# Another written-out order of issue, and another choice of copy engine, in a fused attention, gating and expert kernel

## The chip, the cores and the metric

The kernel runs on one core of a Trainium2 chip. The metric is the device time of one execution in microseconds (us). A core has five engines that each work through an instruction stream of their own, in order: TensorE (PE, with its weight loads shown apart as PEld), VectorE (DVE), ScalarE (ACT), GpSimd (POOL) and SyncE (SP), whose stream here holds the loads. They wait for each other by semaphores.

## What is computed

Three layers follow each other, all in 32-bit floats, for a batch of 2 with 768 tokens, 8 heads of 64 and a model width of 512.

```
attention:  chunks of 32 queries see 16 keys to the left, 8 to the right and 8 memory keys
            a = softmax(q k^T / 8);  x = a v                      -> x[b, s, 512]
gated MLP:  h = gelu(x w_in);  u, v = halves of h
            v_n = (v - mean) / sqrt(var + 1e-6) * g_ln
            v_s = w_sg v_n + b_sg          (over tokens, 768 x 768)
            x1 = x + (u * v_s) w_out
experts:    logits = x1 w_gate; a token takes its argmax expert e, or keeps the expert of
            the token before it, by a second gate
            out = softmax(logits)[e] * relu(x1 w1[e]) w2[e]       (8 experts, 512 x 1024)
```

## The kernel before

The product of two 32-bit matrices is made of three TensorE passes over a high and a low part of each operand (`PASS`, L355), so every operand is split: `split_hi` (L182) is a rounding copy on ScalarE or VectorE, and `split_lo` (L188) a subtraction on VectorE. Attention's own products are plain 32-bit ones.

The work up to the experts consists of small named steps. `at(name, fn)` (L1337) registers them; most are Python generators, and each `yield` ends one piece. `ORDER` (L44 to L98) is a list of 1,021 step names, and the loop at L1440 goes through it: each time a name appears, the next piece of that step is issued. Each engine then executes its own instructions in exactly that order, because the list runs under `manual_schedule` with all five engines. So the list is five queues at once: TensorE's, VectorE's, ScalarE's, GpSimd's, and SyncE's queue of loads. An engine whose next instruction has to wait holds up all that stands behind it.

Step names and their pieces, for batch b and token tile i (128 tokens):

- `lq` loads q and two k tiles (256 KB and two of 192 KB), `q` scales q on ScalarE, `s` makes the scores on TensorE (two mask products, L387, and 32 small ones, L395). `masks` loads the mask rows and builds the mask operands on VectorE (L158 to L171).
- `a..0` takes the row maximum on VectorE (L412), then four exponentials on ScalarE (L415) in two pieces; `a..2` transposes on TensorE (L422) and copies the result out of PSUM (L178 or L180).
- `lv0..`/`lv1..` (three digits) load v (195 KB); `p` multiplies by it (L443), then three VectorE pieces normalise (L451, L453, L456).
- `t` transposes x for 256 tokens and 4 heads (L472), then a high copy and a low subtraction.
- `lv0` to `lv3` (one digit), `lu` and `lo` load the weights w_in and w_out, which arrive as 64-bit floats (two loads of 256 KB each), and `cv`, `cu`, `co` convert them by some nine VectorE pieces each (class `Conv64`, L208; the first, the absolute value, is on ScalarE, L219, or VectorE, L221); `ls`, `cs` do it for w_sg.
- `v`: the matrix product with the v half of w_in (L538, 12 matmuls of 512 columns), gelu, statistics, normalisation and split of one token tile. `u`: the same for the u half (L585). A `v` step of the first batch needs all four `cv` and the `t` steps of its 256 tokens.
- `g..h0` and `g..h1`: the two halves of the token-mixing product (L614), each in two pieces, which fill one PSUM tile `vsp`. `g...1` reads that tile in two pieces (L627) and makes the gated operand. Where `g...1` stands in the list before the last piece of `h1`, TensorE must let VectorE finish that read before it writes the tile on.
- `x`: the product with w_out (L1022) and the addition of x (L1032), stored to DRAM by ScalarE's queue. `lx` and `lg` make the router's logits, `r0` to `r7` and `R..` are the routing of the two batches (some sixty small operations on VectorE in a chain), `RS` gives the places (L942), `G0` to `G2` gather tokens, `XL` builds the first expert tile.
- `consts2` loads small constants: `wgx` in 64-byte rows, `rc`, `g_ln` one number at a time, and `b05`, a row repeated over 128 partitions (393 KB). VectorE then makes eight small operations from them. `rx` makes twelve more. `consts1` is the identity matrix.

`ENG` (L100) gives, for each copy, "a" for ScalarE or "d" for VectorE: AT the copies of `a..2` (24 letters, tile by tile), CB the absolute values and CH the high parts of the 12 weight tiles (cv 0 to 3, cu 0 to 3, co 0 to 3), XH those of `t`, VH of `v`, GH of `g`, SH of w_sg.

All tiles in SBUF come from one pool of 94 slots, and PSUM has eight banks; a new tile waits for the last use of the one whose place it takes. The experts after the list (`moe.run`, L1445) are made of loops whose order for TensorE and SyncE is written out too.

Of the kernel before, what the change touches and what calls it, by code (L numbers as in the profile page):

```python
# [59 lines left out]
lx00.1 s14 a140.0 cu3.0 a120.2 cu2.1 v01.1 a120.2 cu3.0 ls1 lv100 cu3.1 cu3.1 cu3.1 a121.0 v03.0 cu1.1 cu1.1  # L60
cu2.1 cu2.1 cu2.1 a140.0 cu0.1 cu0.1 a121.0 lx01.0 lx01.1 cu3.1 ls4 cu1.1 cu1.1 cu1.1 v03.0 a141.0 cu2.1
a140.0 lv111 v00.1 a130.0 v00.1 ls3 v00.1 a131.2 v02.0 v02.0 lo1 v02.1 a141.0 a130.0 cu2.2 cu0.2 cs7.0 cu2.3
lo3 a131.2 a141.0 cu1.2 v05.0 a140.2 a130.2 a140.2 a141.2 a141.2 cu3.1 v04.0 v03.1 v02.1 lq15 cu1.3 cu0.3 p141
v05.0 v05.1 cu3.1 p111 v03.1 a130.2 lv120 ls0 cu3.2 v03.1 p141 p141 p111 p111 v04.0 p111 v01.1 p110 cu3.3 p140
p141 v04.1 co3.0 v01.1 p100 u02.0 lv101 v01.2 v04.1 p110 v02.1 p110 u02.0 q15 p110 p100 v03.1 v03.1 u02.0 p140
p140 v03.1 v02.1 u02.1 s15 a151.0 a150.0 u00.0 u00.0 p100 ls5 v00.1 v04.1 p140 lv150 p100 v03.1 v03.2 a150.0
v05.1 v04.1 a121.2 a121.2 a150.0 a150.2 a150.2 v05.1 u03.0 v04.1 a151.0 a151.0 u00.0 p121 lv130 v04.1 v04.1
ls8 cs8.0 p101 co2.0 u00.1 p120 p121 p121 p120 lo0 co0.0 v04.2 u00.1 p130 p131 p130 v01.2 p121 p130 u03.0
v02.1 p120 p130 cs6.0 cs6.1 u02.1 u03.0 u03.1 u03.1 lv151 u01.0 u01.0 lx02.0 lx02.1 v00.1 co2.0 v04.2 u02.1
t100 v02.1 u03.1 a151.2 cs8.1 u04.0 v05.1 p120 v00.1 p101 p101 v00.2 v00.2 v05.1 v05.1 v05.1 v01.2 v04.2 cs1.0  # L70
p101 u05.0 v02.1 t100 t100 u05.0 cs7.1 v00.2 a151.2 p151 p150 cs1.1 v02.2 u00.1 p131 u01.0 v02.2 p150 p150
cs5.0 v02.2 u04.0 v05.2 cs4.0 co0.0 v03.2 v03.2 p131 co3.0 g04h0 ls2 g05h0 v05.2 cs3.0 v05.2 p131 cs4.1 co2.1
co2.1 g04h0 g04.1 g04h1 p150 cs5.1 g04h1 cs0.0 t111 cs0.1 cs3.1 co3.1 g05h0 g05h1 g05.1 cs2.0 u04.0 t111 cs2.1
g04.1 u04.1 u04.1 g05h1 g05.1 t111 g01h0 co2.1 co2.1 u04.1 p151 g04.1 g02h0 t101 g00h0 g00h0 co0.1 p151 co1.0
g02h0 u05.0 co0.1 u05.1 p151 g02h1 g01h0 g01h1 g02h1 t110 co1.0 u05.1 co0.1 co0.1 co0.1 co0.1 co2.1 g03h0
co2.1 co2.2 co2.3 t110 g00h1 co1.1 co3.1 co3.1 t101 t101 v11.0 g01h1 u05.1 t121 t110 g03h0 co1.1 co1.1 co1.1
t120 g03h1 g03h1 u01.1 u01.1 t121 co1.1 co1.1 u01.1 co3.1 g05.1 g01.1 g01.1 g01.1 co0.2 t121 g04.1 co0.3 co1.2
g01.1 g00h1 v11.0 co1.2 v11.1 co0.2 co0.3 g04.1 co3.1 co3.1 g00.1 v12.0 v12.0 g00.1 t120 t120 g00.1 g00.1
g03.1 g03.1 v12.1 v11.1 v12.1 v12.1 v11.1 v13.0 v11.1 v11.1 v11.1 v13.0 v13.1 co1.3 v10.0 v11.1 v15.0 v15.0
v12.1 v12.1 v13.1 v13.1 co3.2 g03.1 v14.0 co3.3 g02.1 g01.1 g02.1 v15.1 v15.1 v14.0 g02.1 u12.0 v12.1 v12.1  # L80
co3.2 v10.0 co3.3 u15.0 u15.0 lx12.0 lx12.1 v10.1 v10.1 v15.1 u12.0 v14.1 v15.1 v10.1 v11.2 v12.2 u12.0 v13.1
v15.1 v15.1 v15.1 u13.0 u13.0 v14.1 v14.1 u11.0 v11.2 v11.2 co0.4 u13.0 v13.1 v13.1 u12.1 co2.2 u13.1 u12.1
co0.4 g05.1 g05.1 g00.1 lx10.0 co3.4 co3.4 co2.3 co2.4 co2.4 v10.1 v12.2 v12.2 u10.0 v15.2 co1.3 co1.4 g02.1
g02.1 v10.1 v10.1 v10.1 v14.1 u14.0 g03.1 u15.0 u13.1 g03.1 u10.0 u10.0 u13.1 v10.2 v10.2 co1.4 u11.0 v10.2
lg01.0 u10.1 lg01.1 v14.1 v14.1 zero lg02.0 lg02.1 u11.0 u11.1 u11.1 u12.1 v14.1 lg00.0 v15.2 v15.2 lx10.1
x02h0 x02h1 g15h0 v14.2 v14.2 u14.0 v13.1 g12h0 u10.1 v13.2 v13.2 x02.1 lg00.1 v14.2 v13.2 u11.1 u10.1 g12h0
g12.1 g13h0 g15h0 r0 r0 r0 g13h0 g12h1 u14.0 u14.1 u14.1 g12h1 g15.1 g12.1 g13.1 g11h0 g11h0 g13h1 g12.1 g11h1
r1 u15.1 u14.1 u15.1 r1 r1 r1 g15h1 g14h0 g12.1 r1 g15h1 r1 r2 g14h0 r2 r4 r5 r5 g11h1 u15.1 g15.1 r2 g15.1
x04h0 r5 r5 g12.1 r5 g10h0 pre0 g13h1 g13.1 g13.1 g13.1 g15.1 g10h0 x01h0 r5 x01h1 g15.1 g15.1 g15.1 g11.1
# [1447 lines left out]
```

## Time and profile before

| | us |
|---|---|
| median of 3 runs | 446.39 |
| lowest and highest | 442.04, 447.13 |
| the profiled execution, device time | 445.0 |
| its span, from the first to the last instruction | 443.0 |

Around the span lie 2.0 us. In the span TensorE is busy 412.4 us (93%), its weight loads 361.2 (82%), VectorE 338.6 (76%), ScalarE 207.5 (47%) and GpSimd 43.1 (10%). The page and the trace name an instruction by line, engine, operation and tiles, written as result<-operands. "Idle before" is the time in which the engine stood still just before an instruction, and the arrow names what ended it. Matmuls overlap each other: one of 256 columns lasts 281 ns in the rows but the next starts well before it ends, so a group's mean duration is not what it costs; its busy time is a union of the intervals. The same holds, in a smaller way, for VectorE and ScalarE.

### The profile page before, as it was taken

Reading aid. Unit: us, or ns where it says so; the run is one execution under the profiler, and the core shown is the slowest. Engines: PE = TensorE matmul, PEld = TensorE weight load, DVE = VectorE, ACT = ScalarE, POOL = GpSimd, SP = SyncE. Lnnn points to the kernel's source line nnn. Section 1 sums busy time; section 2 is a strip of 40 time slices with the busy share of each in tenths; the row PEclk is TensorE's granted clock in tenths of the full one; section 3 lists DMA queues with packets and bytes.
Section 4 is the critical chain, followed back from the end, with each engine's and each line's share of the span. In section 5 each row is a group of like instructions: output and inputs, shape, how many; then the busy total and the mean of one; then the engine's idle time right before and its main releaser. Section 6 shows DMA issues by size and latency. Waiting matters only on the chain. (4 is left out here: it accounts for less than half of the span.)

```text
span 443.0 us, 9234 instructions
## 1 busy us (share of the span) xinstructions
PE 412.4 (93%) x3317; PEld 361.2 (82%) x3317; DVE 338.6 (76%) x800; ACT 207.5 (47%) x453; POOL 43.1 (10%) x55
## 2 busy tenths in 40 slices
PE   2887999999999999999799889999999999999991
PEld 1666788998998999998678779889889889988981
DVE  2688999998995889657688997968696696796900
ACT  3696777644232262111020357636656574474510
POOL 1000000110000011000000323001121120000101
PEclk9989999999999999999999999999999999999997
DMA  7999997200000000002705399999897797540101
GB/s 213 307 304 275 319 258 213 80 26 1 1 1 0 1 1 0 2 1 95 277 32 204 112 354 392 391 354 369 250 368 245 256 331 266 189 150 0 44 24 39
DMA packets 43117, 74.74 MB, mean 169 GB/s; under 512 B 6003, under 2 KB 13047, under 8 KB 43066
## 3 DMA queue, kind: packets, MB, share of 16 engines
q1 hardware_dynamic: 38938, 63.87, 44.4%
q0 software_dynamic: 2400, 7.08, 4.5%
q10 hardware_dynamic: 1728, 3.15, 1.9%
q8 instruction: 28, 0.46, 0.4%
q14 instruction: 23, 0.19, 0.1%
HBM read 67.78 MB, written 7.08 MB: 169 GB/s over the span
## 5 line engine op out<-in xcount | busy, mean ns | idle before, releaser
L189 DVE TENSOR_TENSOR we_l<-raw,we_h 128x512 fp32r<-128x512 f32 x160 | 101.9, 688 | 7.1 <-ACT we_h L184 6.1
L184 ACT ACTIVATE we_h<-raw 128x512 fp32r<-128x512 f32 x131 | 73.8, 630 | 15.9 <-DVE s_iw L964 15.4
L1177 PE MATMUL op<-we_h,ht_l 128*128 128x512 f32 x120 | 47.4, 395 | 1.2 <-DVE ht_l L189 1.2
L1177 PE MATMUL op<-we_h,ht_h 128*128 128x512 f32 x120 | 47.8, 398 | 0.0
L1177 PE MATMUL op<-we_l,ht_h 128*128 128x512 f32 x120 | 47.2, 394 | 0.0
L614 PE MATMUL vsp<-sg_h,vh_h 128*128 128x256 f32 x144 | 41.6, 289 | 4.8 <-DVE gtmp L627 4.8
L1132 PE MATMUL hp<-xe_h,we_h 128*128 128x256 f32 x160 | 45.4, 284 | 0.0
L1132 PE MATMUL hp<-xe_l,we_h 128*128 128x256 f32 x160 | 44.9, 281 | 0.0
L1132 PE MATMUL hp<-xe_h,we_l 128*128 128x256 f32 x160 | 44.9, 281 | 0.0
L614 PE MATMUL vsp<-sg_l,vh_h 128*128 128x256 f32 x144 | 40.4, 281 | 0.0
L614 PE MATMUL vsp<-sg_h,vh_l 128*128 128x256 f32 x144 | 40.4, 281 | 0.0
L614 PEld LDWEIGHTS vsp<-sg_h,vh_h 128*128 128x128 f32 x144 | 27.1, 188 | 6.4 <-DVE gtmp L627 6.1
L415 ACT ACTIVATE a<-sc,nm 128x96 f32<-128x96 f32 x96 | 25.4, 368 | 10.7 <-DVE nm L412 8.2
L1132 PEld LDWEIGHTS hp<-xe_l,we_h 128*128 128x128 f32 x160 | 30.1, 188 | 0.0
L1132 PEld LDWEIGHTS hp<-xe_h,we_l 128*128 128x128 f32 x160 | 30.1, 188 | 0.0
L1132 PEld LDWEIGHTS hp<-xe_h,we_h 128*128 128x128 f32 x160 | 30.1, 188 | 0.0
L1186 POOL DMA_INDIRECT out_dram<-o,sidx x15 | 15.8, 1050 | 129.9 <-ACT o L1185 109.4
L1177 PEld LDWEIGHTS op<-we_h,ht_l 128*128 128x128 f32 x120 | 22.5, 188 | 6.9 <-DVE ht_l L189 1.6
L585 PE MATMUL ups<-x_h,in_h 128*128 128x256 f32 x96 | 27.8, 289 | 0.0
L525 ACT ACTIVATE th<-sq 128x512 f32<-128x512 f32 x24 | 15.1, 629 | 26.9 <-DVE sq L522 26.8
L614 PEld LDWEIGHTS vsp<-sg_l,vh_h 128*128 128x128 f32 x144 | 27.1, 188 | 0.1
L614 PEld LDWEIGHTS vsp<-sg_h,vh_l 128*128 128x128 f32 x144 | 27.1, 188 | 0.0
(252 smaller groups left out, 999.5 us busy)
## 6 DMA issues: line engine op xcount, KB each, us to landing
raw<-in_w SPq DMA_DIRECT2D x160, 256.0 KB, 5.2
v<-in_vw SPq DMA_DIRECT2D x24, 195.0 KB, 6.0
k<-in_kw SPq DMA_DIRECT2D x24, 192.0 KB, 5.8
raw_in<-in_w_in SPq DMA_DIRECT2D x16, 256.0 KB, 6.4
q<-in_qT SPq DMA_DIRECT2D x12, 256.0 KB, 6.1
x1d<-x ACTq DMA_DIRECT2D x12, 256.0 KB, 2.5
rsg<-in_w_sgT SPq DMA_DIRECT2D x9, 256.0 KB, 6.8
raw_out<-in_w_out SPq DMA_DIRECT2D x8, 256.0 KB, 6.2
```

The costliest lines, as they stand in the source:

```text
L184: nc.scalar.activation(hi, src, AF.Copy)
L189: nc.vector.tensor_tensor(lo, src, hi.bitcast(F32), ALU.subtract)
L415: nc.scalar.activation(self.a[:, j, :], sc[:, j, :], AF.Exp, bias=nm[:, j : j + 1])
L525: nc.scalar.activation(th, self.sq, AF.Tanh, scale=C2)
L585: nc.tensor.matmul(ps[:, i * 256 : (i + 1) * 256], win_u[k][wa][:, f * 128 : (f + 1) * 128], xT[self.b].at(wb, k, 256 * self.g, 256), star ...
L614: nc.tensor.matmul(self.ps[:, h * 256 : (h + 1) * 256], self.vh[s].hl[wa][:, f * 128 : (f + 1) * 128], rhs_sg(wb, s, self.g), start=(s == ...
L1132: nc.tensor.matmul(ps[:, i * 256 : (i + 1) * 256], self.w[f // 4 * 4 + k][wa][:, f % 4 * 128 : (f % 4 + 1) * 128], self.x[k // 2][wb][:, k ...
L1177: nc.tensor.matmul(self.po[c], h[wa][:, o : o + 128], self.w[8 + k][wb], start=(k == 0 and n == 0), stop=(k == 7 and n == 2),)
L1186: nc.gpsimd.indirect_dma_start(out, bass.IndirectOffsetOnAxis(ap=sidx[:, c : c + 1], axis=0), o, None, bounds_check=NT - 1, oob_is_err=False,)
```

## The change

`ORDER` gets another sequence of the same 1,021 names with the same number of pieces each, and `ENG` other letters. No step is added, removed or changed, and the code of the experts is the same. The start and the end of the list, and `ENG`:

```diff
 ORDER = """
-lq01 masks q01 s01 a010.0 a010.0 consts1 a011.0 a011.0 a011.0 consts2 rx lq00 q00 s00 lq02 q02 lq04 q04 s02
-a021.0 a010.0 a011.2 a011.2 a021.0 a021.0 s04 a001.0 a001.0 a020.0 lv2 cv2.0 a001.0 a001.2 lq03 q03 s03 cv2.0
-cv2.1 a020.0 lv3 lv1 a040.0 a040.0 cv2.1 a020.0 a041.0 a040.0 lq10 a000.0 a000.0 a031.0 a031.0 cv2.1 cv2.1
-cv2.1 a041.0 a030.0 cv1.0 a010.2 cv3.0 cv3.0 a041.0 cv3.1 a001.2 a040.2 a031.0 a040.2 cv3.1 a010.2 q10 a030.0
-a041.2 a031.2 cv3.1 cv3.1 cv1.0 lq05 a000.0 cv3.1 cv3.1 cv1.1 lq11 q05 s10 a101.0 a100.0 a030.0 a000.2 a000.2
-s05 a050.0 a030.2 cv1.1 a021.2 lv000 a101.0 a101.0 cv1.1 a051.0 a031.2 a041.2 lv001 q11 s11 a111.0 cv3.2
-a030.2 cv1.1 p000 p000 a021.2 lv010 a050.0 p001 p000 p000 a050.0 lv041 cv2.1 a110.0 cv3.3 lv011 a101.2 a020.2
-a100.0 a100.0 a100.2 lv030 a051.0 a050.2 p001 p001 a020.2 lv031 p001 a101.2 a110.0 a110.0 p010 a050.2 cv1.1
-cv1.1 p010 p041 p030 p010 a051.0 p010 lv040 p041 lv0 p031 cv2.2 p030 lv020 p030 p041 lv021 a100.2 p030 p031
-p011 lv050 cv2.3 p011 p040 p031 t000 cv0.0 lv051 cv0.0 p040 p040 p040 p011 p011 a110.2 lq13 lq12 a051.2 p041
-p031 a110.2 p020 cv0.1 cv0.1 cv0.1 t001 cv0.1 a051.2 p021 p021 p021 p050 p050 a111.0 t001 a111.0 a111.2 lu0
-cv1.2 p021 p050 p050 p051 p020 t011 t000 t020 q13 lu2 p051 p051 p051 cv0.1 cv0.1 t001 t020 p020 p020 t020
-cv0.2 cv0.3 lq14 a111.2 s13 t021 q12 t000 t010 s12 cv1.3 a130.0 cu0.0 lu1 t011 v01.0 lu3 a121.0 a120.0 t010
-t010 a120.0 a131.0 cu2.0 t011 v01.0 v01.1 lv140 lo2 cu0.0 cu0.1 cu0.1 cu0.1 a131.0 v01.1 v01.1 v01.1 cu1.0 ls6
-t021 cu0.1 t021 a120.0 v00.0 q14 lv121 lv110 cu1.0 ls7 cu1.1 cu2.0 lx00.0 a131.0 lv131 lv141 cu2.1 v00.0 v00.1
...
-g11.1 g11.1 g10.1 g11.1 g10h1 g10h1 r5 g13.1 lg11.0 g11.1 g10.1 g10.1 g10.1 g10.1 pre1 r5 pre2 pre3 x13m0 r6
-x01.1 r6 r6 r6 r6 g14.1 r1 r1 x13m1 g14h1 x13m2 r6 x13m3 lg10.0 g15.1 g14h1 lx11.0 x12m0 g14.1 r6 g14.1 g14.1
-g14.1 lg10.1 lx11.1 x11m0 lg11.1 lg12.0 x12m1 r7 x12m2 lg12.1 x13.1 r3 r5 R1 R1 R1 x05h0 cm0 cm1 x04h1 x04.1
-x02.2 R2 R2 R2 R2 R2 x11m1 x11m2 x05h1 x00h0 R2 R2 R3 R3 R3 x12m3 x12.1 x05.1 RM RA RP x00h1 x03h0 RA x03h1 RP
-RP x01.2 x11m3 RP cm2 RP RP x00.1 RP RP RP RP RA RA RA x03.1 R2 x10m0 RP x10m1 x13.2 x10m2 x10m3 RA RA x04.2
-x00.2 x12.2 RA x11.1 RA x03.2 x11.2 RA x10.1 x14m0 x14m1 RP RP RP RP RP RA RP RP RP RP x14m2 x14m3 RP RP RZ RP
-x15m0 x15m1 RP x15m2 RZ x15m3 R4 RL x05.2 x10.2 RP x14.1 RP G0 RP x15.1 RS RS RE RT RP RT RO RT RT RT x14.2 RE
-XL g15.1 x15.2 G1 cm3 XL XL RA XL G2
+masks lq04 q04 lq03 q03 lq02 q02 s04 a040.0 a040.0 a040.0 s03 a031.0 lq05 q05 a030.0 s02 a041.0 a031.0 a031.0
+a020.0 consts1 a020.0 a020.0 s05 a030.0 a031.2 a050.0 a041.0 a041.0 a021.0 a030.0 lq01 q01 a031.2 a030.2
+a030.2 a020.2 a020.2 lv020 a021.0 a021.0 s01 a010.0 a021.2 a041.2 lv3 cv3.0 cv3.0 lq00 a021.2 p020 q00 cv3.1
+cv3.1 lv1 a050.0 a051.0 a050.0 a050.2 a010.0 a010.0 a041.2 cv3.1 cv1.0 cv1.0 lv2 a051.0 a011.0 a051.0 lv030
+cv3.1 a011.0 lv021 s00 a000.0 a050.2 a010.2 cv2.0 p030 a011.0 cv2.0 lv011 a001.0 cv3.1 cv2.1 cv3.1 cv3.2 cv1.1
+a010.2 a011.2 cv2.1 cv2.1 a051.2 lq10 q10 p030 a040.2 lq12 p020 p030 lv010 p030 a051.2 lv031 a000.0 a000.0 lv0
+p021 cv2.1 cv2.1 s10 lq11 a011.2 p011 p021 cv1.1 cv1.1 cv1.1 a001.0 p021 cv1.1 a001.0 p020 q12 a101.0 a000.2
+a000.2 cv1.1 p020 s12 p021 p031 a101.0 a100.0 cv3.3 a040.2 p011 a100.0 a101.0 a101.2 a121.0 a120.0 p010 p031
+a001.2 p031 lv041 a100.0 cv1.2 a121.0 a121.0 p011 p011 a100.2 t010 q11 a001.2 cv0.0 cv0.0 lv001 a100.2 a120.0
+a120.0 cv2.1 lv050 lv000 cv0.1 cv0.1 a101.2 cv0.1 cv0.1 cv0.1 cv0.1 s11 lv040 p031 a111.0 a111.0 p041 p041
+t011 p041 p041 p001 a110.0 cv1.3 cv0.2 cv2.2 t011 p010 p010 t011 p040 p040 p001 p001 p000 p001 p000 cv2.3 p050
+t001 p040 p040 p050 a110.0 p050 p050 a111.0 a110.0 lq13 q13 p010 p000 t010 t010 t001 t001 a111.2 p000 lv051
+s13 a130.0 a110.2 lq14 q14 t020 t020 p051 p051 p051 lu2 a111.2 t000 p051 s14 t020 cv0.3 t000 cu2.0 t000 a110.2
+a140.0 cu2.0 cu2.1 a131.0 a131.0 a131.0 a141.0 a120.2 a140.0 a120.2 consts2 rx t021 t021 v00.0 v01.0 a141.0
+a141.0 a141.2 lv131 lq15 q15 v01.0 t021 v00.0 v04.0 lv111 a131.2 lv141 v01.1 a140.0 a141.2 v01.1 lu1 cu1.0
...
+g14.1 g11h1 g15h0 r1 g15h0 g14h1 x03.2 g15.1 g15.1 g14h1 g15.1 g15h1 g13h0 u11.1 r1 u11.1 u11.1 g11.1 g11.1
+g11.1 r2 g15.1 r2 g12h0 g12h0 x01h0 g14.1 x05h0 g14.1 u12.1 g11.1 g11.1 g14.1 u12.1 g12.1 g13h0 u12.1 g15h1 r1
+r4 x02.2 g10.1 g13.1 g12h1 pre1 g12h1 r5 r5 r5 g13h1 g13h1 r5 r5 r6 r6 g15.1 g15.1 r5 r1 g10.1 r6 r5 r6 g12.1
+x11m0 pre2 r6 pre3 g15.1 x05h1 g15.1 lg10.0 g14.1 lg12.0 r2 g12.1 cm0 g12.1 g12.1 x13m0 r6 g13.1 x10m0 x10m1
+g15.1 lg10.1 g13.1 g13.1 lx11.0 lx11.1 r5 r3 g13.1 r5 lg11.0 lg11.1 r6 x10m2 lg12.1 x05.1 x10m3 r7 R1 R1 R1
+x01h1 x01.1 x13m1 R2 R2 R2 R2 x11m1 x13m2 x00h0 R2 R2 cm1 R3 R3 x00h1 RM RA x10.1 x12m0 x05.2 x10.2 RA RA RA
+x11m2 RA RA RP RP x13m3 RP RP x01.2 RP RP RP cm2 x04h0 R2 x13.1 x13.2 x00.1 x00.2 x11m3 R2 RP RP RP RL x11.1
+x11.2 R3 x04h1 x04.1 x04.2 RP RP RP RP RP x12m1 x12m2 x12m3 x12.1 x12.2 x15m0 x15m1 x15m2 RA RA x15m3 RA RP RP
+RA RA RP RP RZ RZ x15.1 RP RP RP x14m0 RP RP R4 RP RP x14m1 x14m2 x15.2 RP G0 x14m3 x14.1 x14.2 RO RS RE RS RT
+RT RT RT G1 RE cm3 G2 RA XL XL XL XL RT RP
...
 ENG = dict(
-    AT="adddaaaaadaaaaaaadaaaaaa",
-    CB="addaadaaaaaa",
-    CH="aaadaddadadd",
-    XH="aaaaaaadaaaa",
-    VH="daadaadaadad",
-    GH="daadaadddadd",
-    SH="dadaaadad",
+    AT="aaadadddaaaaaaaaaaaaaaaa",
+    CB="ddddaaaaaaaa",
+    CH="aadaaaadadda",
+    XH="aaaaaaaaaaaa",
+    VH="adaaaaadaadd",
+    GH="aaddaaadaddd",
+    SH="aaaadaaad",
 )
```

## Rows read from the trace of the kernel before

**Rows 1.** Windows of the trace, first 51 us: busy PE, PEld, DVE, ACT, POOL; PEclk, DMA, GB/s
```profile
0.00:10.00 10.00, 3.06 (x36) 1.61 (x36) 2.34 (x11) 3.36 (x9) 2.09 (x11) 1.00 0.69 195
10.00:20.00 10.00, 7.73 (x110) 5.24 (x110) 5.35 (x25) 5.10 (x17) 0.00 (x0) 1.00 0.96 299
20.00:30.00 10.00, 8.59 (x126) 5.92 (x125) 8.72 (x23) 9.17 (x36) 0.00 (x0) 0.83 1.06 336
30.00:40.00 10.00, 8.75 (x191) 7.58 (x189) 9.47 (x34) 8.95 (x28) 0.00 (x0) 1.00 1.05 243
40.00:51.00 11.00, 9.16 (x165) 7.09 (x163) 8.96 (x28) 7.64 (x17) 0.00 (x0) 1.00 1.03 341
```

**Rows 2.** Windows, the later stretches, same columns
```profile
0.00:51.00 51.00, 37.30 (x621) 27.43 (x621) 34.84 (x118) 34.22 (x101) 2.09 (x11) 0.97 0.96 284
51.00:90.00 39.00, 38.77 (x424) 33.94 (x421) 38.02 (x101) 26.54 (x71) 2.10 (x3) 1.00 0.71 188
90.00:120.00 30.00, 28.07 (x256) 27.25 (x255) 26.88 (x66) 11.28 (x23) 2.01 (x3) 1.00 0.04 10
120.00:200.00 80.00, 80.00 (x607) 75.40 (x607) 62.87 (x147) 24.54 (x47) 4.46 (x8) 1.00 0.00 1
200.00:260.00 60.00, 54.91 (x358) 44.88 (x357) 48.52 (x158) 13.81 (x29) 6.42 (x6) 1.00 0.46 160
```

**Rows 3.** Tile vps: ns min/median/max, first and last start; timeline row of the second
```profile
L538 PE MATMUL vps<-in_h,x_h x48: 388/393/503, 51.0 to 148.4; 128*128 128x512 f32 x48
...
53.88 0.39 PE L538 MATMUL vps<-in_h,x_h 128*128 128x512 f32 x1
```

**Rows 4.** Waits of TensorE: total us, times, longest
```profile
PE sc L387 <- DVE mind L167: 5.8, 1, 5.8
...
PE vsp L614 <- DVE gtmp L627: 4.8, 4, 2.7
```

**Rows 5.** The page's DMA issues: count, KB each, us to landing
```profile
v<-in_vw SPq DMA_DIRECT2D x24, 195.0 KB, 6.0
...
k<-in_kw SPq DMA_DIRECT2D x24, 192.0 KB, 5.8
...
q<-in_qT SPq DMA_DIRECT2D x12, 256.0 KB, 6.1
...
raw_in<-in_w_in SPq DMA_DIRECT2D x16, 256.0 KB, 6.4
```

**Rows 6.** Timeline from 8 to 13 us: VectorE and ScalarE waiting for loads
```profile
10.79 0.56 DVE L505 TENSOR_SCALAR b<-b 128x768 f32<-128x768 f32 x1 [1.38 <-DMA b<-in_b_sg]
...
11.48 0.63 ACT L381 ACTIVATE q<-q 128x512 f32<-128x512 f32 x1 [1.22 <-DMA q<-in_qT]
```

**Rows 7.** Groups by line and form: busy us, mean ns, idle before
```profile
L395 PE MATMUL sc<-k,q 64*64 64x96 f32 x384 | 13.7, 290 | 3.4 <-ACT q L381 3.3
...
L422 PE MATMUL at<-ident,a 128*96 128x128 f32 x96 | 15.4, 294 | 2.0 <-ACT a L415 1.4 <-DVE xt L456 0.3 <-DVE x_l L189 0.2
...
L412 DVE TENSOR_REDUCE nm<-sc 128x4 f32<-128x384 f32 x24 | 12.6, 552 | 6.4 <-PE sc L395 6.4
...
L189 DVE TENSOR_TENSOR x_l<-xtp,x_h 128x512 fp32r<-128x512 f32 x12 | 8.2, 686 | 3.9 <-ACT x_h L184 3.9
...
L180 DVE COPY at<-at 96x512 f32<-96x512 f32 x5 | 3.4, 677 | 0.4 <-PE at L422 0.4
...
L186 DVE CAST g_h<-gtmp 128x512 fp32r<-128x512 f32 x6 | 2.5, 417 | 0.1
...
L221 DVE TENSOR_SCALAR cv_in<-raw_in 128x256 uint32<-128x256 uint32 x6 | 1.6, 282 | 0.0
...
L672 DVE CAST rtxb<-wgx 128x16 fp32r<-128x16 f32 x4 | 0.7, 167 | 0.0
```

**Rows 8.** Timeline of TensorE around two late waits
```profile
214.00 0.39 PE L614 MATMUL vsp<-sg_h,vh_h 128*128 128x256 f32 x1 [2.68 <-DVE gtmp L627]
...
248.18 0.46 PE L942 MATMUL inv<-s_eqj,m1v 128*128 128x19 f16 x12 [0.53 <-DVE s_eqj L923]
```

More of the change, by code (lines that the diff above doesn't have):

```diff
@@ L60 @@
[L60 to L89, printed above, removed]
@@ new lines @@
+a140.0 cu2.0 cu2.1 a131.0 a131.0 a131.0 a141.0 a120.2 a140.0 a120.2 consts2 rx t021 t021 v00.0 v01.0 a141.0
+a141.0 a141.2 lv131 lq15 q15 v01.0 t021 v00.0 v04.0 lv111 a131.2 lv141 v01.1 a140.0 a141.2 v01.1 lu1 cu1.0
+lv101 cu1.0 cu2.1 cu2.1 s15 a130.0 p111 v00.1 lv100 v01.1 v01.1 v00.1 cu1.1 a130.0 cu1.1 ls0 a140.2 a121.2
+v01.1 cu2.1 cu2.1 a131.2 lv120 a140.2 v00.1 cu1.1 cu1.1 a121.2 a130.2 lu3 cu3.0 a130.2 lu0 v00.1 p101 lv151
+v00.1 v04.0 lx02.0 cu3.0 a151.0 p111 p111 lx02.1 cu1.1 v00.1 a151.0 cu1.1 ls1 p100 p100 lv130 p111 p101 cu1.2
@@ new lines @@
+cu3.1 v04.1 v03.0 cu3.1 p120 cu0.0 lx00.0 cu0.0 p101 a151.0 a151.2 p100 cu0.1 cu3.1 p101 v04.1 v04.1 cu2.1
+v03.0 cu1.3 v00.1 v00.2 cu0.1 cu0.1 cu0.1 cu2.2 lv110 p120 lx01.0 a150.0 lx01.1 ls3 ls2 p110 cu3.1 ls8 cs3.0
+cu3.1 v02.0 lx00.1 v03.1 v03.1 p110 p110 p110 p100 cu0.1 cu0.1 lv121 cu3.1 t101 v05.0 v03.1 t101 cu2.3 a150.0
+cu0.2 v05.0 t100 a150.0 t101 cu0.3 p131 cu3.2 cu3.3 p130 p130 p131 cs8.0 p130 p130 a151.2 p121 ls5 lo1 v04.1
+v04.1 v04.1 lv150 p131 u00.0 u00.0 ls4 v01.1 v02.0 p121 p121 lo3 p120 p120 p121 v02.1 v03.1 v01.1 v01.2 co3.0
@@ new lines @@
+co1.0 cs1.0 lo2 lv140 u03.0 v00.2 p131 co2.0 v04.1 u00.0 v02.1 v03.1 cs4.0 v02.1 v05.1 lo0 u05.0 co2.0 cs4.1
+u03.0 v05.1 ls7 cs7.0 u00.1 ls6 a150.2 a150.2 u03.0 u05.0 v05.1 v05.1 p150 co0.0 p151 cs8.1 u03.1 u01.0 v02.1
+t100 u03.1 u00.1 p151 u03.1 v00.2 cs6.0 v03.1 p151 t100 p150 p150 p150 u01.0 u04.0 v03.1 cs3.1 co1.0 co2.1
+co3.0 p151 u04.0 u04.0 v03.2 v02.1 v01.2 p140 p141 p140 v03.2 v04.2 p140 p141 u05.0 u00.1 u02.0 v02.1 co3.1
+v11.0 co1.1 co1.1 v02.1 v05.1 v05.1 u01.0 u02.0 co1.1 v04.2 cs7.1 v05.1 v05.2 v02.2 p141 p141 v10.0 cs2.0
@@ new lines @@
+cs2.1 co2.1 v02.2 cs5.0 v05.2 cs6.1 v01.2 v02.2 g05h0 p140 v03.2 g04h0 v05.2 v04.2 g04h0 cs0.0 v10.0 v10.1
+g04.1 v10.1 v10.1 v10.1 co0.0 cs0.1 v11.0 g05h0 g05h1 cs1.1 u04.1 g04h1 g04h1 v11.1 u04.1 u04.1 g00h0 co1.1
+zero v10.1 cs5.1 u02.0 g01h0 g04.1 g01h0 co0.1 co2.1 co2.1 g04.1 g03h0 g03h0 g03h1 co1.1 co1.1 g01h1 co0.1
+co3.1 u01.1 co0.1 g04.1 g04.1 g00h0 g05.1 v11.1 co3.1 v11.1 v11.1 u01.1 co2.1 u01.1 g00h1 co3.1 g02h0 g00h1
+g02h0 co1.2 co0.1 co1.2 u05.1 u05.1 g05h1 g00.1 g00.1 g05.1 u05.1 g05.1 v10.1 co0.1 co0.1 co1.3 g02h1 u02.1
@@ new lines @@
+g01h1 t120 g01.1 t110 g01.1 g03h1 t110 co0.2 t110 co0.2 v10.1 g05.1 v10.2 g03.1 g02h1 u02.1 u10.0 g03.1 u02.1
+co3.1 t121 t121 co0.3 co0.3 t111 g03.1 t111 g00.1 u10.0 t111 t120 v12.0 t120 t121 v15.0 v12.0 co2.1 co2.2
+v12.1 co2.3 v12.1 v12.1 v11.1 g05.1 u11.0 v15.0 v15.1 v15.1 v15.1 v13.0 v12.1 g00.1 v13.0 v15.1 v13.1 v14.0
+v13.1 v11.1 v12.1 co1.3 g02.1 g02.1 g03.1 g02.1 g02.1 v13.1 v13.1 co3.1 g00.1 lx12.0 co2.2 g01.1 co3.2 v11.1
+v10.2 v12.1 v11.2 co3.3 v15.1 v15.1 v15.1 v14.0 v14.1 v14.1 g01.1 u14.0 v12.1 lx12.1 v10.2 g03.1 u14.0 co0.4
@@ new lines @@
+u15.0 u15.0 v11.2 v11.2 g02.1 co2.3 u11.0 v15.2 co3.2 co0.4 co3.3 lx10.0 u14.0 x02h0 u14.1 x02h1 u13.0 u13.0
+v15.2 lx10.1 x02.1 u14.1 v14.1 u15.0 v14.1 u15.1 u15.1 v13.1 x03h0 u15.1 g01.1 v12.2 v12.2 u14.1 x03h1 v12.2
+v13.1 v13.1 v14.1 v14.1 v13.2 co3.4 co1.4 co1.4 v14.1 co2.4 g11h0 co2.4 x03.1 u12.0 u10.0 v13.2 u10.1 u10.1
+v14.2 v14.2 u13.0 co3.4 u10.1 g14h0 v15.2 lg00.0 u12.0 v13.2 v14.2 g14h0 lg01.0 lg01.1 u13.1 u13.1 g10h0 g10h0
+g10.1 lg02.0 g11h0 lg02.1 lg00.1 pre0 r0 r0 u13.1 u11.0 g10h1 g10h1 r0 r1 u12.0 g11h1 r1 g10.1 g10.1 r1 r1
```

## The prediction

> **What bounds the kernel now.** I read the windows first, then the waits of TensorE, then the list itself. In the windows look at the PE column against the length of each window. From 51 to 90 us TensorE is busy 38.77 of 39, from 120 to 200 all of 80 [rows 2]. Nothing that only reorders work can gain there, since the same matmuls remain. What is left to gain is its idle time: 51.00 - 37.30 = 13.7 us before 51 us, 30.00 - 28.07 = 1.9 from 90 to 120, and 60.00 - 54.91 = 5.1 from 200 to 260 [rows 2], 20.7 us in all. 51.0 us is where the first large product, of a v step, starts [rows 3]; from there TensorE always has a store of large products.
>
> Before that point three resources share the blame. VectorE is idle 12.3 of the first 20 us (20 - 2.34 - 5.35), then busy 27.15 of the 31 us that follow (8.72 + 9.47 + 8.96) [rows 1]. The DMA share is 1.03 to 1.06 from 20 us on, at 243 to 341 GB/s, but 0.69 at 195 GB/s in the first ten [rows 1]. TensorE starts only at 5.8 us, when VectorE has built the mask operand [rows 4]. The first 20 us starve all engines; afterwards VectorE and the loads run nearly full.
>
> **The start of the list.** At present the loads of `consts2` stand behind the first q, so VectorE waits for `b05` until 10.79 us and the second q is scaled only at 11.48 [rows 6]. In the new list `masks` comes first of all, then q and k of tiles 4, 3, 2, 5, 1; the weights begin after 3,402 KB, and `consts2` comes behind 11,947 KB. What this gives is worked out from three sides.
>
> Loads: by the sizes [rows 5] I add up the list. Now, up to the last scores in front of the first v product (`s12`): ten tiles of q and k, 6,400 KB, twelve v, 2,340, six weight halves, 3,072, and constants, 592: 12,404 KB. After, up to `s14`: eleven tiles, 7,040, twelve v, 2,340, four weight halves, 2,048, the mask, 7: 11,435 KB, or 11.7 MB. At about 300 GB/s, the level of the windows from 10 us on [rows 1], that is 39 us. Starting after about 2 us, the last k lands near 41 and the v product can start at 43 to 44, after `s14` and six transposes. This is the lower end.
>
> TensorE: eleven score steps and 17 transposing steps instead of ten and 16 lie ahead of the first v product. One score step is 13.7 / 12 = 1.14 us, one transposing step 15.4 / 24 = 0.64 [rows 7], so 1.8 us of its work moves from behind that point to before it, into time now idle.
>
> VectorE: it has done 34.84 us of work by 51 us [rows 2]. For the same point the new list needs three more row maxima (12.6 / 24 = 0.53 each), four more absolute values, as CB puts all of cv on VectorE (1.6 / 6 = 0.27 each), and two more subtractions (8.2 / 12 = 0.68): +4.0. The operations of `consts2` and `rx` move behind it: `b05` 0.56 [rows 6] and three kinds at 0.7 [rows 7], -2.7. So 36.1 us of work. Its idle time in the first 20 us falls, as five tiles of attention are ready by then: ten maxima, 5.3, three copies of AT at 0.68 (the four d of the new AT all lie early), 2.0, the masks, about 1, and the start of cv3, about 1.5, make 9.8 us of work, so 10.2 idle instead of 12.3. From 20 us to the v product it had 3.9 idle [rows 1]; I take 2, as loads of weights come later but attention is further ahead. 36.1 + 10.2 + 2 = 48.3 us. VectorE is then the last of the three, ahead of the loads (44).
>
> So the v product starts at 48.3 instead of 51.0, 2.7 us earlier, with 1.8 us more done: 4.5 us.
>
> A rule about the constants: the windows show 195 GB/s in the first ten microseconds and 299 in the next [rows 1]. The Trainium skill (DMA: Bandwidth & Descriptors, Why small descriptors are slow) says that each descriptor costs a fixed overhead, which tells most on short ones; by it the 64-byte and 4-byte rows of `consts2` are slow wherever they stand, and moving them back only moves the loss to a time when the queue is full. By that rule 10 x (1 - 195 / 299) = 3.5 us of transfer time would fall on `lv131`, `lq15` and `lu1`, and the sum would be unchanged as long as TensorE has the first two v products; if instead the slow start is just the queue filling, the first 20 us stay as starved as now and the sum is 2 us smaller.
>
> **Behind the first v product.** `consts2` now makes VectorE wait in mid-list for `b05`. Behind it stand `rx`, the subtraction of `t021` and the gelu of v. Loads take about 6 us to land [rows 5], and with the queue full this one can be late too. TensorE has v00 and v01 in front of anything that needs `t021`'s subtraction: the first product now starts at 51.0, the second at 53.88 [rows 3], so two are 5.8 us of cover. I cost the wait at nothing, between 0 and 3 us.
>
> The letters: 31 d become 24. AT and XH lose one each from PSUM (0.68), CH two, VH one, GH one and SH two from SBUF (0.42 each), CB gains one weight tile of two pieces (0.28) [rows 7]: -1.4 - 2.5 + 0.6 = -3.3 us on VectorE, and about as much more on ScalarE, which is busy 11.28 of 30 us and less from 90 us on [rows 2]. So VectorE runs some 3 us further ahead in the middle. The 1.9 us idle there, where it was busy 26.88 of 30 [rows 2], should mostly go: -1.5 us, between -1.9 and +2.
>
> The end: the same pattern that costs 4.8 us now, TensorE waiting to write `vsp` on until VectorE has read it [rows 4], is there in seven products of the old list and in seven of the new one. The longest, 2.68 us [rows 8], came of rank operations in VectorE's queue. The routing chain of the second batch starts (`R1`) with 90 matmuls of `x` left now and 84 in the new list, and TensorE waits for its end 0.53 us now [rows 8]. Six matmuls are half a product of 2.9 us, 1.4 us less cover; but `cm0` with two weight subtractions, 0.69 each like those of [rows 7], leaves the chain. I cost the end at nothing, between -3 and +4. The experts are the same.
>
> Sum on the profiled execution: 445.0 (span 443.0 and 2.0 around it) - 4.5 - 1.5 = 439.0. The median of the three runs is 1.4 above that execution, so I forecast 440.4.
>
> **Rivals.** (A) VectorE is not last and the loads decide: v starts at 44, 7.0 us earlier, plus 1.8, plus 1.5 to 3 later: 10.3 to 11.8, 434.6 to 436.1. For it: VectorE's pieces for the weights can fill every gap. Against: it ran 27.15 of 31 us already. (B) The start is gained but waits later take it back: all seven `vsp` reads late at 4.8 / 4 = 1.2 us each, 8.4 instead of 4.8, and 2 us for `b05`: 440.4 + 5.6 = 446.0, no change. For it: large products that come earlier find VectorE less far; against: its queue is shorter. (C) Slower: VectorE decides and is held up ahead of the first v product. cv0, the last weight, comes in one piece behind its load (8,345 KB into the list, 31 us at 300 GB/s), and everything of attention behind it waits. If VectorE's idle time before the v product is not 12.2 but 20 us, v starts at 56.1, 5.1 us later, less 1.8: 449.7. It decides from 52.8 us on (51.0 + 1.8), that is from 16.7 us of idle time, against 16.2 now. (D) The order does nothing, as TensorE's idle time merely sits elsewhere: that is B's number.
>
> **How the numbers follow.** The forecast 0.50, A 0.25, B (with D) 0.16, C 0.09. The likeliest gives 440.4. The range goes from 432.5, two microseconds below A, to 448.5, most of the way to C. A measurement of this kernel can tell about 2% (8.9 us) from no change: below 437.5 lie nearly all of A and a few hundredths of the forecast, 0.26; above 455.3 only the tail of C, 0.04; within, 0.70.
>
> **What would show it.** Right: the first v product (L538) at 46 to 50 us; VectorE idle about 10 us in the first 20; TensorE's first instruction near 4.5 us; idle time of TensorE before the v product down from 13.7 to about 9; the window from 120 to 200 still full. Wrong: a v product after 52 us, a wait of several microseconds at L505 with TensorE idle behind it, or new waits of `vsp` or of L942 above 5 us together.

## The result, and the profile after

The changed kernel takes 440.37 us (median; 437.00 to 441.79) where the kernel before took 446.76 beside it: ratio 0.9883, 95% interval 0.9837 to 0.9930. Timed again later it takes 438.64 against 444.30: 0.9859 (0.9812 to 0.9906). So it is about 6 us faster (5.7 and 6.4 by the medians), 1.2 to 1.4%. The profiled execution took 441.71 us with a span of 439.9, 3.1 us less than before.

The windows of the changed kernel, with the columns of [rows 1] and [rows 2]:

```profile
0.00:10.00 10.00, 4.95 (x68) 3.15 (x68) 1.65 (x7) 3.90 (x8) 1.17 (x9) 1.00 0.76 242
10.00:20.00 10.00, 8.55 (x151) 5.85 (x144) 7.02 (x16) 9.29 (x35) 0.00 (x0) 1.00 1.07 348
20.00:30.00 10.00, 7.59 (x89) 5.61 (x91) 7.90 (x26) 7.17 (x24) 0.98 (x2) 0.68 1.04 267
30.00:40.00 10.00, 9.30 (x190) 7.34 (x192) 9.32 (x31) 7.56 (x25) 0.00 (x0) 0.98 1.00 257
40.00:51.00 11.00, 9.24 (x165) 7.30 (x168) 9.54 (x30) 7.22 (x19) 0.00 (x0) 0.84 0.95 261
0.00:51.00 51.00, 39.65 (x647) 29.26 (x650) 35.42 (x106) 35.14 (x106) 2.15 (x11) 0.90 0.96 275
51.00:90.00 39.00, 38.14 (x373) 32.78 (x362) 35.29 (x111) 26.32 (x69) 1.75 (x3) 1.00 0.75 207
90.00:120.00 30.00, 30.00 (x276) 28.53 (x275) 26.36 (x64) 12.64 (x25) 2.23 (x3) 1.00 0.00 1
120.00:200.00 80.00, 80.00 (x603) 76.17 (x602) 61.78 (x142) 24.67 (x46) 4.71 (x8) 0.98 0.06 18
200.00:260.00 60.00, 57.48 (x389) 47.90 (x389) 52.33 (x166) 16.50 (x34) 6.31 (x6) 1.00 0.46 161
```

Read the first column after the length. TensorE's idle time fell from 13.7 to 11.35 us in the first 51, from 1.9 to 0 between 90 and 120, and from 5.1 to 2.5 between 200 and 260; 51 to 90 lost 0.6. That is 6.2 us less idle time, but the span fell by only 3.1. The difference stands in the PEclk column: 0.90 over the first 51 us against 0.97, and 0.98 from 120 to 200 against 1.00. A busy TensorE at half clock is not a gain. By that column the clock took back up to 5.2 us (0.07 of 51 and 0.02 of 80), and the spans say 3.1: such a sum gives an upper bound.

TensorE's waits, to be read against [rows 4] (total us, times, longest):

```profile
PE sc L387 <- DVE mind L167: 3.1, 1, 3.1
PE xp L443 <- DMA v<-in_vw: 2.4, 1, 2.4
PE xp L443 <- DVE x_l L189: 1.4, 1, 1.4
...
PE ups L585 <- DVE xt L456: 0.9, 1, 0.9
...
PE inv L942 <- DVE s_eqj L923: 0.7, 1, 0.7
```

The wait for the mask came down from 5.8 to 3.1. The waits for `vsp`, 4.8 us before, are in no row at all: the pattern of [rows 8] is gone. Two early waits, for a load of v and for a subtraction, are new.

The first v product (tile vps, as in [rows 3]) and the operation on `b05` that [rows 6] showed waiting, with first and last start:

```profile
L538 PE MATMUL vps<-in_h,x_h x48: 387/394/502, 52.0 to 151.5; 128*128 128x512 f32 x48
```

```profile
L505 DVE TENSOR_SCALAR b<-b x1: 558/558/558, 53.7 to 53.7; 128x768 f32<-128x768 f32 x1
```

v starts at 52.0, not at 48.3 as forecast, and later than the 51.0 of before. L505 has no wait: moving the constants back cost nothing here. The windows show 242 instead of 195 GB/s in the first ten microseconds and 261 instead of 341 from 40 to 51. The Trainium skill (DMA: Bandwidth & Descriptors, Why small descriptors are slow) gives each short descriptor a fixed cost, and these two rates fit that. They do not show it: the loads of `consts2` are issued from 42.2 to 44.2 us here, but the rate is 257 from 30 to 40 us already, and the kernel before has 243 there without these rows [rows 1]. No engine waited for them.

The stretches where the clock fell, TensorE alone (length, busy, PEclk, DMA share, GB/s):

```profile
22.00:24.00 2.00, 0.00 (x0) 0.92 1.09 277
24.00:26.00 2.00, 1.78 (x20) 0.50 1.00 305
26.00:28.00 2.00, 2.00 (x10) 0.50 1.02 251
28.00:30.00 2.00, 2.00 (x23) 0.50 1.01 287
...
44.00:46.00 2.00, 2.00 (x14) 0.54 0.93 229
...
174.00:176.00 2.00, 2.00 (x10) 0.50 0.00 0
```

0.50 is the lower of the two levels, 1.2 of 2.4 GHz. From 22 to 24 us TensorE waited for v; behind that wait it worked at half clock up to about 30 us. So three questions: is the early part worth what was forecast, where does the rest of the gain come from, and what do the letters do?

### The profile page after: what moved, and what is told of

Read it like the earlier page. It is cut to its first block, busy times and chain, and to the rows that moved or that the text cites. A ratio compares the mean times of both kernels' runs of the same rounds, so it can differ in the third digit from the quotient of the medians.

```text
span 439.9 us, 9222 instructions
## 1 busy us (share of the span) xinstructions
PE 416.3 (95%) x3317; PEld 364.9 (83%) x3317; DVE 335.5 (76%) x794; ACT 211.0 (48%) x459; POOL 43.0 (10%) x55
## 5 line engine op out<-in xcount | busy, mean ns | idle before, releaser
L585 PE MATMUL ups<-x_l,in_h 128*128 128x256 f32 x96 | 27.2, 284 | 0.0
```

The source lines that it names most:

```text
L585: nc.tensor.matmul(ps[:, i * 256 : (i + 1) * 256], win_u[k][wa][:, f * 128 : (f + 1) * 128], xT[self.b].at(wb, k, 256 * self.g, 256), star ...
```

## The experiments

Ratios are to the kernel before, timed beside each kernel. Four kernels have other line numbers: in the two that splice the lists near the first v product, and in the two that change the order or the engines alone, every line named is one less.

**Order and engines apart.** The first keeps the new `ORDER` with the old `ENG`, the second the reverse.

```diff
-    AT="aaadadddaaaaaaaaaaaaaaaa",
-    CB="ddddaaaaaaaa",
+    AT="adddaaaaadaaaaaaadaaaaaa",
+    CB="addaadaaaaaa",
...
```

> New order of issue, old choice of engines (31 copies on VectorE instead of 24). My theory: the order carries most of the gain and the choice of engines about 1.5 us, by about 3 us less work on VectorE between the first v product and 120 us. So this kernel gains 4 to 5 us against the kernel before (ratio about 0.990), and TensorE idles about 2 us more between 51 and 120 us than in the changed kernel. Rival: the choice of engines matters as much as the order; then this one gains under 2.5 us (ratio above 0.994).

442.79 against 444.44: 0.9965 (0.9928 to 1.0002), the rival's number: the order alone gives 1.65 us, not 4 to 5, and its interval takes in no gain at all. From 51 to 120 us TensorE idles 0.9 us more than in the changed kernel, not 2.

```diff
 ORDER = """
-masks lq04 q04 lq03 q03 lq02 q02 s04 a040.0 a040.0 a040.0 s03 a031.0 lq05 q05 a030.0 s02 a041.0 a031.0 a031.0
+lq01 masks q01 s01 a010.0 a010.0 consts1 a011.0 a011.0 a011.0 consts2 rx lq00 q00 s00 lq02 q02 lq04 q04 s02
...
```

> Old order of issue, new choice of engines. My theory: about 1.5 us faster than the kernel before (ratio about 0.997), by the idle time of TensorE from 90 to 120 us (1.9 us before) going to under 0.5 us; the first v product stays at 51 us within 1 us. Rival (the engines matter as much as the order): 3 us or more (ratio 0.993 or less). A third possibility: it loses, since the old order was made for the old engines (ratio above 1.0).

449.37 against 444.44: 1.0110 (1.0051 to 1.0170), a loss of 5 us: the third possibility. The letters are worth about 4 us in the new order (0.9965 to 0.9859 or 0.9883) and cost 5 in the old one: they have no price of their own. And the middle, from 90 to 120 us, with the new letters alone and with the new order alone (TensorE):

```profile
90.00:120.00 30.00, 28.38 (x301) 1.00 0.04 11
...
90.00:120.00 30.00, 30.00 (x276) 1.00 0.00 1
```

The idle time there went by the order, not by VectorE's letters.

**The early and the late part of the list, spliced at the first v product.**

```diff
 consts2 rx t021 t021
-v00.0 v01.0 a141.0 a141.0 a141.2 lv131 lq15 q15
+lu0 cu0.0 lu1 v01.0 lu3 v01.0 v01.1 lv140
...
```

> New list up to its first v product, then the remaining pieces in the sequence of the old list; new engines. Theory of the prediction: the gain lies ahead of the first v product, so this kernel gains 4 us or more against the kernel before (ratio 0.991 or less). Rival, suggested by the profile of the changed kernel: the gain comes of the waits for vsp between 180 and 230 us, which the new sequence of the later part has not; then this kernel gains at most 2 us (ratio above 0.9955) and TensorE shows the vsp waits of the kernel before again (about 4.8 us).

444.88 against 444.44: 1.0008 (0.9973 to 1.0043). No gain at all, with the same 257 names up to the first v product as in the changed kernel. Three views of it, each with one or two lines: TensorE's waits, its timeline at the longest, and the windows there (TensorE alone):

```profile
PE vsp L613 <- DVE gtmp L626: 5.1, 4, 2.9
```

```profile
213.63 0.39 PE L613 MATMUL vsp<-sg_h,vh_h 128*128 128x256 f32 x1 [2.92 <-DVE gtmp L626]
```

```profile
214.00:216.00 2.00, 2.00 (x12) 0.70 0.92 237
216.00:218.00 2.00, 2.00 (x8) 0.50 0.92 322
```

The `vsp` waits are back, and behind the longest one the clock falls, which costs TensorE up to 1.5 us more (0.97 over 50 us). Only the order behind the first v product separates this kernel from the changed one, so behind this start the new order is worth 1.25 to 1.5%, 5.5 to 6.5 us. What a list loses because its halves were not made for each other is in that number too. The clock stayed at 1.00 up to 51 us in this profile, and v starts at 49.7:

```profile
L537 PE MATMUL vps<-in_h,x_h x48: 387/395/507, 49.7 to 146.9; 128*128 128x512 f32 x48
```

```diff
 a130.0 cu0.0 lu1 t011
-v01.0 lu3 a121.0 a120.0 t010 t010 a120.0 a131.0
+a121.0 a120.0 a121.0 a121.0 a120.0 a120.0 t011 t010
...
```

> Old list up to its first v product, then the remaining pieces in the sequence of the new list; new engines. Theory of the prediction: only about 1.5 us faster than the kernel before (ratio about 0.997). Rival (the later part carries the gain): 3 to 5 us faster (ratio 0.993 to 0.989), with no wait for vsp in the list of TensorE's waits, while the first v product stays near 51 us.

446.22 against 444.44: 1.0046 (1.0013 to 1.0079), a miss for both. No `vsp` wait is in its profile, but v starts at 58.6 us: the cut left early pieces in front of it, and the new letters stand in the old early list. As a test of the late part this splice was no good; the pair further down has a better cut.

**One read of `vsp`, in the old kernel.** The only edit is one name moved, the first `g14.1`; it passes thirteen names, not twelve.

```diff
-g10.1 g10.1 g10.1 g10.1 pre1 r5 pre2 pre3 x13m0 r6 x01.1 r6 r6 r6 r6 g14.1 r1 r1
+g10.1 g10.1 g14.1 g10.1 g10.1 pre1 r5 pre2 pre3 x13m0 r6 x01.1 r6 r6 r6 r6 r1 r1
```

> The kernel before, old list and old engines, with one VectorE read of vsp moved ahead of twelve names (two pieces of g10.1, rank operations, an addition of x). Theory that the waits for vsp are on the path: the wait of 2.7 us near 214 us goes to under 0.6 us, and the kernel is 2 to 3 us faster than before (ratio 0.993 to 0.9955). Rival: what is gained there is given back in the routing chain, whose operations VectorE does 0.5 us later, or by a wait at L942: under 1 us faster (ratio above 0.998).

441.30 against 444.30: 0.9921 (0.9889 to 0.9953), 3.0 us by the medians and 3.5 by the ratio. TensorE's waits, where [rows 4] had 4.8 with a longest of 2.7:

```profile
PE vsp L614 <- DVE gtmp L627: 2.1, 3, 0.9
```

The wait of 2.68 us was on the path, and no later wait took its place: L942 still waits 0.5 us. Between 180 and 230 us TensorE is busy 49.33 us, where the kernel before has 46.66:

```profile
180.00:230.00 50.00, 46.66 (x344) 1.00 0.26 90
```

That is 2.7 us, in line with the medians. The spans of the two profiles differ by more, 4.9 us, and 2.0 of that has nothing to do with the read: v starts at 49.0 in this profile and at 51.0 in [rows 3], with the same list up to there. TensorE's waits of the kernel before have a row that this profile has not:

```profile
PE xp L443 <- issue: 1.8, 1, 1.8
```

It is a wait at 42.95 us for which the profile shows no releaser. One name of 1,021 gives about half of what the whole change gives. The other three late reads were not moved.

**The changed kernel again, and two edits of it.**

> The changed kernel as it is, once more, timed beside the three others. Both theories expect a ratio to the kernel before of 0.985 to 0.991. The theory that the profiled execution's late first v product (52.0 us) came of the lower clock alone expects it at 49 to 50 us here if the clock stays at its upper level before it, as it was in the kernel with the early part alone (49.7 us).

438.64 against 444.30, 0.9859 as said. The clock fell again ahead of the first v product, so this run does not settle the late start. Its windows (TensorE alone) are the cleanest to set beside [rows 2]:

```profile
0.00:51.00 51.00, 41.33 (x660) 0.93 0.97 275
51.00:90.00 39.00, 38.14 (x362) 1.00 0.76 207
90.00:120.00 30.00, 30.00 (x275) 1.00 0.01 1
120.00:180.00 60.00, 60.00 (x444) 1.00 0.00 1
180.00:230.00 50.00, 50.00 (x387) 1.00 0.32 106
230.00:260.00 30.00, 27.59 (x167) 1.00 0.63 226
```

v starts at 50.6 us here. Idle time against before: -4.0, +0.6, -1.9, 0 and, from 180 to 260, -2.7 (200 to 260 in [rows 2]); together -8.0. The clock gives back up to (0.97 - 0.93) x 51 = 2.0. That makes -6.0, and the spans are 443.0 and 437.0. The agreement is closer than the method: 0.01 of clock is 0.5 us here, and for the first profile the same sum gives -1.0 where the spans differ by 3.1.

```diff
-u14.1 x03h1 v12.2 v13.1 v13.1 v14.1 v14.1 v13.2 co3.4 co1.4 co1.4 v14.1
+u14.1 co3.4 x03h1 v12.2 v13.1 v13.1 v14.1 v14.1 v13.2 co1.4 co1.4 v14.1
```

> The changed kernel with one block of 8 matmuls of 16 columns moved ahead of 12 matmuls of the x product, so that 24 of them in a row become 8 and 16 apart, as in the kernel before. Theory: the fall of the clock near 174 us follows those 24; with them apart it stays away, which gives 1.0 to 1.6 us against the changed kernel (the fall cost 1.5 us in its profile, and need not come each time). Rival: the fall near 174 us has nothing to do with them; then no change within 0.5 us, or a fall at the same place.

437.93 against 444.30: 0.9849 (0.9801 to 0.9897). No fall near 174 us, but the unedited kernel's second profile has none either. It cannot be told from the changed kernel; whether the 24 in a row bring the fall stays open (below).

```diff
-cv3.1 lv1 a050.0 a051.0 a050.0 a050.2 a010.0 a010.0 a041.2 cv3.1 cv1.0 cv1.0 lv2 a051.0 a011.0 a051.0 lv030
+cv3.1 lv030 lv1 a050.0 a051.0 a050.0 a050.2 a010.0 a010.0 a041.2 cv3.1 cv1.0 cv1.0 lv2 a051.0 a011.0 a051.0
```

> The changed kernel with one load of v (195 KB) issued ahead of two weight tiles (1,024 KB). Theory: TensorE's wait of 2.4 us for that v at 21.8 us goes or falls below 1 us, and with it the fall of the clock behind it: the first v product at 47 to 49 us, 1.5 to 3 us faster than the changed kernel. Rival A: VectorE, which gets those weights 0.7 us later, then sets the first v product: under 0.5 us faster. Rival B: the clock falls all the same, elsewhere in the first 51 us, and the time stays within 1 us of the changed kernel.

439.06 against 444.30: 0.9884 (0.9839 to 0.9929). The wait for v is gone, but TensorE then waits 1.9 us at 26.5 us, before the next product with v, for ScalarE's copy at L178, the clock falls between 28 and 30 us, and v starts at 50.7. That is rival B.

**Letters and parts with a better cut.** The late letters alone, in the old order:

```diff
-    CH="aaadaddadadd",
+    CH="aaadaaadadda",
-    VH="daadaadaadad",
+    VH="adaaaaadaadd",
...
```

> Old order of issue; of the new choice of engines only the letters for work behind the first v product (high parts of cu and co, v, g and w_sg, one absolute value of cu), the letters for attention and cv as before. All new letters in the old order cost 4 to 5 us. Theory: that loss lies ahead of the first v product (v started at 53.0 us there), where letters and list belong together; so this kernel is within 1.5 us of the kernel before (ratio 0.9965 to 1.0035). Rival: the later letters do the harm (the longer wait for vsp, the fall of the clock behind it): ratio 1.007 or more.

446.91 against 444.20: 1.0050 (1.0022 to 1.0078), between the two. About half of the letters' loss is late: `vsp` waits 5.1 us instead of 4.8, and the clock is 0.97 from 180 to 230 us. This kernel and the one with the new early part differ in little but the early order and its letters: 446.91 and 444.88. That would put the early part at 2.0 us, as an estimate: the two were timed at different times, and the intervals of their ratios, 1.0022 to 1.0078 and 0.9973 to 1.0043, overlap.

The last two are cut near 100 us, where the two lists have issued nearly the same; each step keeps the letter of the list that issues its copy.

```diff
 co2.1 co2.1 g04h0
-g04.1 g04h1 p150 cs5.1 g04h1 cs0.0 t111 cs0.1
+t101 t101 t101 co1.0 p151 p151 p150 cs3.1
...
```

> Old list with its letters up to its 524th name (about 100 us), then the remaining pieces in the sequence of the new list, with the new letters for steps whose copies are issued there. Theory, after the earlier runs: the later part carries most of the gain, since it lets no read of vsp come late; 3.5 to 5.5 us faster than before (ratio 0.9875 to 0.992), no wait for vsp above 0.3 us between 180 and 230 us. Rival (the prediction's): 1.5 us or less (ratio above 0.9965).

442.44 against 444.20: 0.9944 (0.9910 to 0.9978), 1.8 us by the medians and 2.5 by the ratio: less than expected and more than the rival had it. No `vsp` wait for a read is left; a wait of 1.4 us of a v product, right behind the cut, takes part of it.

```diff
 v05.2 v04.2 g04h0
-cs0.0 v10.0 v10.1 g04.1 v10.1 v10.1 v10.1 co0.0
+u02.0 u02.1 u02.1 u02.1 cs1.1 co0.0 g04.1 g04h1
...
```

> New list with its letters up to its 538th name (about 100 us), then the remaining pieces in the sequence of the old list with the old letters. Theory, after the earlier runs: 0 to 2 us faster than before (ratio 0.9955 to 1.0), with the wait for vsp of some 3 us near 214 us still there. Rival (the prediction's, 4.5 us for the early part): ratio 0.991 or less.

446.94 against 444.20: 1.0066 (1.0038 to 1.0095), slower than both theories had it. Its waits of TensorE:

```profile
PE vsp L614 <- DVE gtmp L627: 4.8, 4, 2.7
...
PE wops L294 <- DVE rtgb L672: 0.7, 1, 0.7
...
PE vps L538 <- ACT woTout L289: 0.7, 1, 0.7
```

The old late order keeps its 4.8 us, and two waits appear that neither list has by itself. The halves do not add up: -0.6% and +0.7% alone, -1.2 to -1.4% together. So no half has a price that holds with another half beside it. A list is matched along its whole length.

**Keeping TensorE at work in its early waits.**

```diff
             xp = bank([128, 4, DV], "xp")
+            if self.n == "030":
+                for _ in range(14):
+                    nc.tensor.matmul(xp.rearrange("p a b -> p (a b)"), mind[0], mrow[:, : 4 * DV], start=True, stop=True)
...
-cv0.2 cv2.2 t011 p010 p010 t011 p040
+cv0.2 t011 p010 p010 t011 cv2.2 p040
```

> The changed kernel with 14 idle matmuls of 260 columns (their result is overwritten by the product that follows) in TensorE's wait for v at 21.8 us, and one VectorE copy of a weight moved behind the subtraction that TensorE waits for at 41.3 us. Theory: the falls of the clock ahead of the first v product follow these two waits, and they ate 1.5 to 3 us of what the new start had gained; with TensorE kept at work the granted clock stays at its upper level up to 50 us, v starts at 49 to 50 us, and the kernel is 1 to 2.5 us faster than the changed kernel (ratio to before 0.979 to 0.984). Rival A: the clock falls there all the same, and the ratio stays at 0.984 to 0.989. Rival B: the idle matmuls delay the work behind them, v starts after 51 us without any fall of the clock: ratio above 0.989.

437.57 against 443.40: 0.9881 (0.9857 to 0.9905). First the window of TensorE, then the v product (its line is three higher here), then VectorE's window up to it:

```profile
0.00:51.00 51.00, 41.42 (x683) 1.00 0.99 279
```

```profile
L541 PE MATMUL vps<-in_h,x_h x48: 387/394/503, 48.4 to 147.8; 128*128 128x512 f32 x48
```

```profile
0.00:48.40 48.40, 35.91 (x108) 1.00 0.99 280
```

The clock stays up to 51 us and v starts at 48.4, 2.2 us earlier than in the changed kernel's second profile. But the time cannot be told from the changed kernel's: the spans differ by only 0.9, since in this profile the clock fell at 170.6 us and took up to 1.7 back (0.66, 0.50 and 0.99 in the windows of 2 us from 170). Nor are the 2.2 us all the clock's: the run has two edits, and with no edit of the start and the clock at 1.00 v began at 49.7, in the kernel with only the early part new. So v comes early where the clock stays up, but whether the edits kept it up, and which of them, is not shown by one profile, and a gain in time is not shown either (rival A's ratio, without its fall of the clock). No kernel of these beats the changed one measurably.

## Why the prediction was right, and where not

440.4 us was forecast and 440.37 measured. A hit that close is luck: four executions spread from 437.00 to 441.79, and the second timing gave 438.64. The sum of -6.0 is right (5.7 and 6.4 measured), and so is its direction. Its terms are not: two wrong sizes made up for each other.

**The start of the list (forecast -4.5).** This step failed in size: about -2, by the second profile's windows (-4.0 of idle time, 2.0 given back by the clock) and by the pair 446.91 and 444.88. Even that hangs on the profile it is set beside. With the old start and its letters v began at 51.0, 49.0, 50.5 and 51.6 us in four profiles (the kernel before, one read moved, the late letters, the late part alone); beside the second of them the same sum is -0.2, beside the last -4.3. With the new start v began at 49.7, 50.6, 52.0, 52.1 and 52.5 us in five. So v does not come 2.7 us earlier, and no run shows the 1.8 us of work ahead of it by themselves. Part of the old idle time is the wait of 1.8 to 2.1 us without a releaser, near 43 us in the kernel before: it is in five of six profiles with the old start and in none of eight with the new one. The prediction had no term for it, and its cause is open.

The work was counted right: VectorE had done 36.42 us of it by 52 us, forecast 36.1. Two things are wrong in 36.1 + 10.2 + 2 = 48.3. VectorE idles 11.2 to 11.6 us in the first 20 in those five profiles, not 10.2. Where the clock stayed up, with only the early part new, that alone is the miss: 36.16 + 11.62 + 1.92 = 49.7. The other is a term that the sum lacked, TensorE's clock. [rows 1] had shown it, at 0.83 from 20 to 30 us. The changed list lets TensorE wait 2.4 us for v at 21.8 us and 1.4 at 41.5, and behind these it ran at half clock for some us; in that profile VectorE idles 4.25 us between 20 and 52, not 2. In the five profiles with the new start the mean clock over 51 us was 1.00, 0.93, 0.90, 0.90 and 0.90, in the order of the starts above. The 48.4 of the run with idle matmuls is not the 48.3 of the sum: it took two edits, and its terms are 35.91 + 11.4 + 1.1. The signs said so: 52.0 is outside the 46 to 50 named as right and at the edge of "after 52 us" named as wrong; TensorE idled 11.35 us, not 9; it began at 3.1 us, not 4.5.

**Behind the first v product.** `b05` at nothing: right. The middle, -1.5: right in size (-1.9 and, new at 82 us, a wait for `xt` of 0.9; 51 to 90 us lost 0.6), wrong in cause, as the order alone removes it. The letters as a price of their own, 3.3 us less work for VectorE, was a wrong notion: they gain 4 us or lose 5 by the list that they stand in.

**The end (forecast 0, between -3 and +4).** Here is the rest of the gain. The step argued that the same pattern is there seven times in both lists. It counted names; what decides is whether VectorE reaches the read before TensorE reaches the write, and in the new list it does for all 24 reads of `vsp`. The idle time from 180 to 230 us, 3.3 us, is gone (46.66 us busy before, 50.00 after); with it goes the fall of the clock that followed the longest wait in four of the five profiles that have it (the kernel before's own is the fifth). Some of it comes back from 230 to 260, which leaves 2.7. Moving one read in the old kernel gave 3.0 to 3.5 us, so that wait was on the path.

**The rivals.** A did not come: v started at 50.6 and 52.0 us, not 44. One earlier load of v gave nothing, though TensorE does wait 2.4 us for that load, so the loads have a part. Nothing was given back by `vsp` (B), and v came before the 52.8 us from which C would have decided. So the range held, and the likeliest case came true in its sum, with about 2.5 us too much in the first term and 2.7 too little in the last.

## What to carry to other kernels

Where an engine must finish reading a tile before another may write it on, look up in the trace what stands ahead of that read in its engine's list: one name moved gave 3.0 to 3.5 us here, where the whole change gave 6. A wait of TensorE of 2 to 3 us can cost more than its length, since the work behind it may run at half clock (22 to 30 us in the changed kernel); compare profiles by the clock column before comparing starts. One profile of each kernel is not enough: the old start alone put v anywhere from 49.0 to 51.6 us. Engine letters and an order of issue are tuned to each other, so changing one alone says nothing about the other.
